# Inverse transform read back in long rows, DK reload ahead of weights and U^T, first dense blocks moved behind the first Z

## The chip, the cores and the metric

One core of a Trainium2 chip runs the whole program in one launch. The metric is device microseconds of one execution; lower is better.

## The reference

`reference` runs a gated layer forward and takes the gradient of its output against `grad_out`. With `u` of shape 2048 x 448 (positions l, channels d), N = 256 states and F = 1792 hidden units it computes:

```python
g = sigmoid((u * gate_w).sum(-1))
K[d, l] = Re sum_n C[d,n] * exp(dt[d] * A[d,n] * l) * dt[d] * B[d,n]     # l rounded to bf16
a = irfft(rfft(pad(u)) * rfft(pad(K))) [:2048] + u * Dskip               # causal convolution
b = relu(u @ w1 + b1)**2 @ w2 + b2
out = g * a + (1 - g) * b
_out, _vjp = jax.vjp(_f, u, A_re, A_im, B_re, B_im, C_re, C_im, log_dt, Dskip, w1, b1, w2, b2, gate_w)
```

Outputs are `out` and the 14 gradients. The gradient of the convolution kernel, dK, is a correlation of `u` with `g * grad_out`; it is needed only at the bf16-rounded positions, where several l share one position. From dK come the gradients of A, B, C and dt, by sums over powers of exp(dt A).

## The kernel before

**Transforms.** The convolutions are FFTs in two matrix stages, with a trip through DRAM between the stages. `fwd1` and `fwd2` make the spectra of u and of g * grad_out, `cprod` their product, and `inv1p` (L292, store L296) the first inverse stage of dK. Its result goes to the scratch tensor `hd[0]`, laid out as (64 * k1 + 16 * g + 8 * hp + x, d), where g is 0 to 3, hp 0 or 1 and x 0 to 7.

**dK sum (L690 to L719).** `hd[0]` is read back into four tiles `hss` of 128 partitions x 3584 elements (two in buffer D16, two in P14). `load_hs(q)` (L319) reads, for one q, the x values 2q and 2q+1 of all four g: four rows of 1792 bytes per partition. SP issues the half hp = 1 and ACT the half hp = 0. Then 160 matmuls (L713) with 32-column weights from `ct["Ew"]` and `Ew2` add the terms into five PSUM tiles (and one row of a sixth). A key (x8, g, e, gr) says which x and g a matmul reads, which PSUM tile e it adds to, and which 32-partition strip gr of it: `tile_position=(0, 32 * gr)`. The keys are sorted with x8 first, so runs of four or five matmuls for one g (and almost always gr = g) follow one another, g by g.

**DK trip (L717 to L735).** ACT copies the PSUM tiles to `stA`, `stB`. Thirteen small stores to `dk_d` alternate between the queues of SP and POOL (GpSimd). Five loads and one row on each of the two queues then read `dk_d` into `DK` (buffer K28), one copy per 64 partitions, each load waiting for the stores it reads.

**Weights.** `w1` goes to buffer U16 by three DMAs on SP (L697, L700), issued behind the `hd[0]` loads; `w2` (L1029) goes to D16 on POOL; the first two blocks of U^T (`load_ut`, L568) go to SB on POOL, behind a memset of `XB`.

**Main loop (L960 to L1006).** c runs over NCH = 14 chunks of 32 channels. `build_x` (L773, L774, L777) and `build_y` (L784, L785, L787) double tables of powers on DVE, the latter in two halves; `expand_x`, `expand_y` (L807 to L814) on ACT spread the factors they need from the loads `recx`, `recy` (L798, L802). `tables_t` and `turn_yt` transpose on PE and copy on ACT (L871, L883), `load_yt` transposes by DMA on SP (L890). `kgen` (L844) makes K. `dk_chunk(c)` (L895, L896, on ACT) copies the chunk's part of DK to `DKs`. One round later `back_z` multiplies DKs with the Y tables on PE (L913, copy L917 on ACT) and `back_p` multiplies the result Z with the X tables on DVE (L933) and sums on PE (L942). Of each half of `build_y` from c = 1 on, the second is ordered behind the first half's `back_p`.

**Dense part.** `hidden(lb, jp)` computes two 128-row blocks of the hidden layer: eight matmuls (L584, L587) from w1 and U^T, two Relu (L589) and a Square (L591) on ACT, and a store (L595). `project` (L1021, L1022) is the second layer. At the end of round c = 0 six hidden blocks are traced, into the PSUM tags NT[4:6] ("X" and "S").

**What sets the order.** Every engine runs its own instructions in a fixed order, worked out at build time from the trace order, priorities and dependencies. `tc.issue_after(ins)` adds an order edge behind `ins` on the same engine, without a wait for its completion. DMAs of one queue are issued in order.

Of the kernel before, what the change touches and what calls it, by code (L numbers as in the profile page):

```python
# [19 lines left out]
P = 128  # L20
L, D, N, F = 2048, 448, 256, 1792
# [6 lines left out]
NG = 4  # L28
# [306 lines left out]
def kernel(ctx, tc, A_u, A_A_re, A_A_im, A_B_re, A_B_im, A_C_re, A_C_im, A_log_dt, A_Dskip,  # L335
# [3 lines left out]
    nc = tc.nc  # L339
    V, S, G_, T_ = nc.vector, nc.scalar, nc.gpsimd, nc.tensor  # L340
# [9 lines left out]
    hd = [dscr(f"hd{i}", SPN) for i in range(3)]  # L350
# [5 lines left out]
    dk_d = dscr("dk_d", 769 * D)  # L356
# [10 lines left out]
    K = Ker(tc, pool, psum)  # L367
# [30 lines left out]
    for h in range(2):  # L398
        for g in range(NG):
            src = bass.AP(tensor=u2.tensor, offset=u2.offset + (16 * g + 8 * h) * D, ap=[[64 * D, 32], [1, 8 * D]])  # L400
# [65 lines left out]
    NT = ["N0", "N1", "N2", "N3", "X", "S"]  # L466
# [75 lines left out]
    e, im = (x.rearrange("p c w -> p (c w)") for x in (E0, Tt))  # L542
# [24 lines left out]
    def load_ut(lb):  # L567
        G_.dma_start(UTb[lb % 2].rearrange("p a l -> p (a l)"), bass.AP(tensor=UT_d, offset=lb * P * 2048, ap=[[2048, P], [1, 2048]]))  # L568
# [4 lines left out]
    def hidden(lb, jp, banks, ring):  # L573
        nonlocal nti, rxi
        ub = UTb[lb % 2]
        rx = ring[rxi % len(ring)]
        rxi += 1
        pss = []
        for j in (2 * jp, 2 * jp + 1):
            ps = K.ps(banks[nti % len(banks)], [P, 512])  # L580
            nti += 1
            pss.append(ps)
            for dt in range(DT - 1):
                T_.matmul(ps[:], lhsT=w1w[:, dt, j * P:j * P + P], rhs=ub[:, dt], start=(dt == 0), stop=False, skip_group_check=True)  # L584
        for k in range(2):
            h, j = slice(64 * k, 64 * k + 64), 2 * jp + k
            T_.matmul(pss[k][:], lhsT=w1w[h, 3, j * P:j * P + P], rhs=ub[h, 3], start=False, stop=True, tile_position=(64 * k, 0), skip_group_check=True)  # L587
        for k in range(2):
            S.activation(rx[:, 512 * k:512 * k + 512], pss[k][:], ACT.Relu, bias=b1_f[:, 2 * jp + k:2 * jp + k + 1])  # L589
        if jp < 6:  # L590
            S.activation(SB[:, 4096 + 1024 * jp:5120 + 1024 * jp], rx, ACT.Square)  # L591
        else:
            for k in range(2):
                S.activation(hsq(12 + k), rx[:, 512 * k:512 * k + 512], ACT.Square)
        G_.dma_start(bass.AP(tensor=rT_d, offset=2 * jp * P * L + 512 * lb, ap=[[L, P], [P * L, 2], [1, 512]]), rx.rearrange("p (k l) -> p k l", k=2))  # L595
# [14 lines left out]
    for rb, _, _ in psets:  # L610
        xs, ys, _, _ = fields(rb.rearrange("p (c r) -> p c r", c=4))
# [76 lines left out]
        Ew2 = SB[:, 10752:10752 + NW2]  # L688
        nc.sync.dma_start(Ew2, nc.inline_tensor(cs["Ew2"].astype(ml_dtypes.bfloat16), name="c_Ew2").ap())
    hsD, hsP = K.t("D16", [P, 8192]), K.t("P14", [P, 7168])  # L690
    hss = [b[:, 3584 * i:3584 * i + 3584].rearrange("p (g x d) -> p g x d", g=4, x=2) for b in (hsD, hsP) for i in range(2)]
    for q in range(4):
        lhs = K.load_hs(hd[0], q, hss[q], True)
    w1v = K.t("U16", [P, 8192])
    w1w = w1v[:, 0:7168].rearrange("p (a f) -> p a f", a=DT)
    with tc.issue_after(lhs.ins):
        nc.sync.dma_start(w1w[:, 0:3], bass.AP(tensor=B_w1.tensor, offset=B_w1.offset, ap=[[F, P], [P * F, 3], [1, F]]))  # L697
    for h in range(2):
        with tc.issue_after(lhs.ins):
            nc.sync.dma_start(w1w[64 * h:64 * h + 64, 3], bass.AP(tensor=B_w1.tensor, offset=B_w1.offset + 384 * F, ap=[[F, 64], [1, F]]))  # L700
    KB = K.t("K28", [P, 14336])
    DK = KB[:, 0:VA * D].rearrange("p (a d) -> p a d", d=D)
    G_.memset(KB[:, 12 * D:VA * D].bitcast(fp32), 0.0)
# [1 line left out]
    psE = K.psF()  # L705
    tiles = [psS[0], psS[1], psS[2], psS[3], psE[:, 0], psE[:, 1]]
    first, last = {}, {}
    for k, (x8, g, e, gr) in enumerate(ekeys):
        first.setdefault((e, gr), k)
        last[e, gr] = k  # L710
    for k, (x8, g, e, gr) in enumerate(ekeys):
        lt = ct["Ew"][:, 32 * k:32 * k + 32] if k < 128 else Ew2[:, 32 * k - 4096:32 * k - 4064]
        T_.matmul(tiles[e][32 * gr:32 * gr + 32, 0:D], lhsT=lt, rhs=hss[x8 // 2][:, g, x8 % 2, :], start=(k == first[e, gr]), stop=(k == last[e, gr]),  # L713
                  tile_position=(0, 32 * gr), skip_group_check=True)
    stA, stB = (K.t("st", [P, 4, D], bufs=2) for i in range(2))
    for i in range(4):
# [2 lines left out]
    S.copy(stB[0:1, 1], psE[0:1, 1, 0:D])  # L719
    pieces = [(2 * e, 2, 128 * e, 1, stA[:, e]) for e in range(4)] + [(8, 4, 512, 2, stB[:, 0])]  # L720
    n_ = 0
    ldk = {}
    for (a0, na, r0, st_, src) in pieces:
        for al in range(na):
            qe = (nc.sync, G_)[n_ % 2]
# [3 lines left out]
    for cpy in range(2):  # L729
        qe = (nc.sync, G_)[cpy]  # L730
        with tc.issue_after(ldk[cpy].ins):
            for (a0, na, r0, st_, _) in pieces:
                qe.dma_start(DK[64 * cpy:64 * cpy + 64, a0:a0 + na].rearrange("p a d -> p (a d)"),
                             bass.AP(tensor=dk_d, offset=r0 * D, ap=[[na * D, 64], [1, na * D]]))
            qe.dma_start(DK[64 * cpy:64 * cpy + 1, 12], bass.AP(tensor=dk_d, offset=768 * D, ap=[[D, 1], [1, D]]))  # L735


    YA = K.t("Y16", [P, W2, 2, 64])
# [2 lines left out]
    XWs = [XB[:, 4096 * k:4096 * k + 4096].rearrange("p (t w a r) -> p t w a r", t=2, w=W2, a=NA) for k in range(2)]  # L741
    for k in range(2):
        mx = G_.memset(XB[:, 4096 * k:4096 * k + 4096].bitcast(fp32), 0.0)
    with tc.issue_after(mx.ins):
        load_ut(0)
        load_ut(1)
    Fv = K.t("F17", [P, 8704])
    Vt = Fv[:, 0:4096]
    PRY = Fv[:, 4096:5376].rearrange("p (l w t d) -> p l w t d", l=5, t=2, d=2)
# [148 lines left out]
    def back_z(c, YTs, gs):  # L898

        nonlocal zi  # L900
        cc = c % GC
        DKc = DKs[:, c % 2]
        zb = Zr[zi % 2].rearrange("p (s t g n) -> p s t g n", t=2, s=2, g=2)
        zi += 1
        for gg, g in enumerate(gs):
            psz = K.psF()
            for s in range(2):
                for par in (1, 0):
                    for ii in range(4):
                        i = 2 * ii + par  # L910
                        m = (1 + par) * NA
                        for t in range(2):
                            T_.matmul(psz[32 * ii:32 * ii + m, t, 256 * s:256 * s + 256],  # L913
                                      lhsT=DKc[64 * t:64 * t + 64, s, g, 2 * ii:2 * ii + 1 + par].rearrange("p i a -> p (i a)"),
                                      rhs=YTs[g][64 * t:64 * t + 64, :, i, :], start=True, stop=True, tile_position=(64 * t, 32 * ii),
                                      skip_group_check=True)
            S.copy(zb[:, :, :, gg].rearrange("p s t n -> p t s n"), psz[:].rearrange("p t (s n) -> p t s n", s=2))  # L917
        return zb
# [46 lines left out]
    for c in range(NCH + 1):  # L965
        z01 = z23 = None
        if c < NCH:
            with tc.issue_after(ay.ins) if ay is not None else nullcontext():
                seeds_x(c)
            ax = build_x(c)  # L970
            if c + 1 < NCH:
                load_rx(c + 1)
            XTs[c] = [tables_t(c, 0)]
            YTs[c] = []
        if c > 0:
            z01 = back_z(c - 1, YTs[c - 1], (0, 1))
        if c < NCH:
            XTs[c].append(tables_t(c, 1))
        if c > 0:
            z23 = back_z(c - 1, YTs[c - 1], (2, 3))  # L980
        for half in range(2):
            if c < NCH:
                ay = build_y(c, half, ax if half == 0 else ap or ay)
                if half == 1:
                    k_out(c, kgen(c))
                for g in (2 * half, 2 * half + 1):
                    YTs[c].append(turn_yt(c, g, ("S", "N3")) if c == 0 else turn_yt(c, g) if g == 3 or c == NCH - 1 else load_yt(c, g))
                if c + 1 < NCH:
                    if half == 0:
                        lry = load_ry(c + 1)  # L990
                        lry1 = lry if c == 0 else lry1
                        expand_x(c + 1)
                        if c == 0:
                            expand_y(1, 0, 4)
                    elif c == 0:
                        expand_y(1, 4, 5)
                    else:
                        expand_y(c + 1)
                if half == 0:
                    dk_chunk(c)  # L1000
            ap = None
            if c > 0:
                ap = back_p(c - 1, XTs[c - 1][half], (z01, z23)[half], (2 * half, 2 * half + 1), ay if c < NCH else None)
        if c == 0:
            for jp in range(6):
                hidden(0, jp, NT[4:6], [w1v[:, 7168:8192], Fv[:, 2048:3072], Fv[:, 3072:4096]])  # L1006

    ring = [w1v[:, 7168:8192], Fv[:, 2048:3072], Fv[:, 3072:4096], P2[:, 0:1024], P2[:, 1024:2048]]
    ni = 0
# [15 lines left out]

    w2v = K.t("D16", [P, 8192])
    w2n = w2v[:, 0:FT * D].rearrange("p (j d) -> p j d", d=D)
    with tc.issue_after(lry1.ins):
        G_.dma_start(w2n, bass.AP(tensor=B_w2.tensor, offset=B_w2.offset, ap=[[D, P], [P * D, FT], [1, D]]))  # L1029
    hidden(0, 6, NT[0:3], ring)  # L1030
    for lb in range(4):
# [410 lines left out]
```

## Time and profile before

| | us |
|---|---|
| runs | 958.52, 960.26, 954.6, 958.17 |
| median of the four | 958.35 |
| profiled execution | 958.52 |
| its span | 956.4 |
| PE busy | 712.3 (74% of the span) |
| DVE busy | 671.3 (70%) |
| ACT busy | 586.1 (61%) |
| POOL busy | 191.7 (20%) |

The span runs from the first to the last instruction of the core; 2.1 us of the execution's time lie around it. Engines: PE is TensorE (PEld its weight loads), DVE VectorE, ACT ScalarE, POOL GpSimd, SP SyncE (here only a DMA queue). "L713" is line 713 of the kernel before. Tiles are written by the first letters of their names, so "S" can be the buffer SB or a PSUM tag, and "K<-dk_d" is the DK reload. The mean granted TensorE clock is 0.831 of full speed.

### The profile page before, as it was taken

What the parts mean: (1) busy time and instruction counts of PE and PEld (TensorE: products, weight loads), DVE (VectorE), ACT (ScalarE), POOL (GpSimd) and SP (SyncE); (2) the same over time, 40 slices, a digit from 0 to 9 for tenths busy, and PEclk for the clock granted to TensorE, in tenths of its full rate; (3) what the DMA queues carried; (4) which work ended last, traced back from release to release, by engine and by line L of the source; (5) the groups of instructions that cost most, each with busy time, mean ns of one, the idle gap of its engine ahead of it and who ended that gap; (6) DMA issues with size and microseconds to landing.
All of it is one profiled execution on the core that took longest, in us unless ns stands there. A gap on an engine that the chain in (4) does not pass through costs nothing. (4 is left out here: it accounts for less than half of the span.)

```text
span 956.4 us, 18969 instructions
## 1 busy us (share of the span) xinstructions
PE 712.3 (74%) x7625; PEld 342.8 (36%) x7657; DVE 671.3 (70%) x1152; ACT 586.1 (61%) x936; POOL 191.7 (20%) x327
## 2 busy tenths in 40 slices
PE   3346675735878888787987886988958889868975
PEld 1112222214344443344543442443323345423443
DVE  4387885786499999899986899854238662288800
ACT  3335757725997869689676755664327645437544
POOL 2141000113202122021202311232300022433310
PEclk9675555668869899899966998899968879868998
DMA  9976486797526756436843976469998995879531
GB/s 187 264 236 228 167 310 244 285 314 218 132 66 124 154 135 136 110 84 148 191 88 89 234 152 141 127 156 287 355 330 265 274 293 177 215 231 288 152 105 45
DMA packets 161887, 184.98 MB, mean 193 GB/s; under 512 B 90963, under 2 KB 137464, under 8 KB 160872
## 3 DMA queue, kind: packets, MB, share of 16 engines
q1 hardware_dynamic: 111958, 82.38, 35.4%
q0 software_dynamic: 20480, 61.51, 19.9%
q10 hardware_dynamic: 29362, 39.88, 12.9%
q8 instruction: 60, 0.98, 0.4%
q14 instruction: 27, 0.22, 0.1%
HBM read 90.58 MB, written 73.13 MB: 171 GB/s over the span
## 5 line engine op out<-in xcount | busy, mean ns | idle before, releaser
L933 DVE TENSOR_TENSOR P<-R 128x2048 bf16<-128x2048 bf16 x42 | 49.5, 1218 | 23.7 <-ACT R L917 20.9
L1159 PEld LDWEIGHTS <-S 128*128 128x128 bf16 x448 | 43.8, 103 | 60.6 <-issue 18.5
L917 ACT CAST R<-psF 128x1024 bf16<-128x1024 f32 x56 | 57.5, 1026 | 12.4 <-PE psF L913 12.4
L1021 PE MATMUL psN<-D,S 128*128 128x448 bf16 x208 | 53.5, 391 | 6.4 <-ACT S L591 6.3
L1159 PE MATMUL psF<-U,S 128*128 128x448 bf16 x224 | 51.7, 381 | 2.1 <-ACT S L1154 2.0
L913 PE MATMUL psF<-R,S 64*32 64x256 bf16 (+1 forms) x1344 | 37.9, 296 | 9.7 <-DMA R<-Y 4.6
L584 PE MATMUL psN<-S,U 128*128 128x512 bf16 x119 | 37.6, 420 | 9.7 <-ACT F L589 4.8
L1084 PE MATMUL psN<-S,U 128*128 128x512 bf16 x113 | 35.6, 425 | 8.6 <-ACT D L1089 6.9
L773 DVE TENSOR_TENSOR X<-X,F 128x512 bf16<-128x512 bf16 (+1 forms) x70 | 37.4, 534 | 4.8 <-ACT F L807 2.9
L207 DVE CAST K<-psN 128x448 bf16<-128x448 f32 x36 | 21.6, 620 | 27.2 <-PE psN L255 27.1
L1153 PEld LDWEIGHTS <-S 128*128 128x128 bf16 x448 | 30.0, 103 | 28.3 <-issue 11.6
L784 DVE TENSOR_TENSOR K<-K,F 128x2048 bf16<-128x2048 bf16 (+3 forms) x42 | 36.4, 866 | 5.4 <-ACT F L812 3.8
L1097 POOL DMA_DIRECT2D dhT_d<-D x28 | 20.2, 720 | 91.1 <-DVE D L1096 90.9
L785 DVE TENSOR_TENSOR F<-K,F 128x2048 bf16<-128x2048 bf16 (+3 forms) x42 | 35.9, 855 | 3.0 <-ACT F L814 3.0
L784 DVE TENSOR_TENSOR Y<-Y,F 128x2048 bf16<-128x2048 bf16 (+3 forms) x42 | 36.3, 864 | 1.5
L787 DVE TENSOR_TENSOR K<-K,F 128x2048 bf16<-128x2048 bf16 (+3 forms) x42 | 36.3, 865 | 1.3
L787 DVE TENSOR_TENSOR Y<-Y,F 128x2048 bf16<-128x2048 bf16 (+3 forms) x42 | 36.3, 865 | 1.3
L774 DVE TENSOR_TENSOR F<-X,F 128x512 bf16<-128x512 bf16 (+1 forms) x70 | 36.8, 526 | 0.6
L785 DVE TENSOR_TENSOR F<-Y,F 128x2048 bf16<-128x2048 bf16 (+3 forms) x42 | 35.9, 854 | 0.3 <-ACT F L814 0.3
L1021 PE MATMUL psN<-S,D 128*128 128x448 bf16 x168 | 35.7, 361 | 0.0
L1354 DVE SCALAR_TENSOR_TENSOR F<-psN,Y 128x448 bf16<-128x448 f32 x16 | 9.9, 618 | 36.0 <-PE psN L329 36.0
L883 ACT COPY M<-psX 128x1024 bf16<-128x1024 bf16 x26 | 26.6, 1022 | 14.0 <-PE psX L882 13.9
(378 smaller groups left out, 1946.7 us busy)
## 6 DMA issues: line engine op xcount, KB each, us to landing
sp<-K ACTq DMA_DIRECT2D x8, 896.0 KB, 8.5
hd<-st ACTq DMA_DIRECT2D x16, 448.0 KB, 2.9
dhT_d<-D POOLq DMA_DIRECT2D x28, 256.0 KB, 5.2
R<-sp SPq DMA_DIRECT2D x8, 896.0 KB, 9.1
S<-rT_d POOLq DMA_DIRECT2D x14, 512.0 KB, 5.3
R<-hd SPq DMA_DIRECT2D x16, 448.0 KB, 6.1
S<-dhT_d POOLq DMA_DIRECT2D x14, 512.0 KB, 4.5
rec_d<-F ACTq DMA_DIRECT2D x2, 1920.0 KB, 9.1
```

The costliest lines, as they stand in the source:

```text
L584: T_.matmul(ps[:], lhsT=w1w[:, dt, j * P:j * P + P], rhs=ub[:, dt], start=(dt == 0), stop=False, skip_group_check=True)
L773: V.tensor_tensor(out=hi4, in0=lo, in1=bcast_dims(pr, [0, (None, n), 1]), op=ALU.mult)
L774: V.tensor_tensor(out=Vv.rearrange("p (x a r) -> p x a r", x=2 * W2, r=2), in0=lo, in1=bcast_dims(pi, [0, (None, n), 1]), op=ALU.mult)
L784: V.tensor_tensor(out=hi, in0=lo, in1=bcast_dims(pr, [0, (None, n // 2), 1]), op=ALU.mult)
L785: V.tensor_tensor(out=Vv.rearrange("p (x a q) -> p x a q", x=rows, q=2), in0=lo, in1=bcast_dims(pi, [0, (None, n // 2), 1]), op=ALU.mult)
L787: return V.tensor_tensor(out=T4[:, :, :, n:2 * n], in0=T4[:, :, :, n:2 * n], in1=V4, op=ALU.add)
L913: T_.matmul(psz[32 * ii:32 * ii + m, t, 256 * s:256 * s + 256], lhsT=DKc[64 * t:64 * t + 64, s, g, 2 * ii:2 * ii + 1 + par].rearrange("p i ...
L917: S.copy(zb[:, :, :, gg].rearrange("p s t n -> p t s n"), psz[:].rearrange("p t (s n) -> p t s n", s=2))
L933: lastp = V.tensor_tensor(out=pr.rearrange("p s t g n -> p s t (g n)"), in0=zv, in1=(xb if r == 0 else rev_dim(xb, 2)), op=ALU.mult)
L1021: lastm = T_.matmul(ps[:, 0:D], lhsT=hblk[j][:, P * tt:P * tt + P], rhs=ws[:, j, :], start=(w == 1 and j == 0), stop=(j == FT - 1))
L1084: T_.matmul(ps[:], lhsT=w2Tw[:, jp, dt, j % 2], rhs=dblk[:, dt], start=(dt == 0), stop=False, skip_group_check=True)
L1159: lastm = T_.matmul(ps[:, 0:width], lhsT=hh[:, t, :], rhs=(DB2[:, t, :] if w == 0 else U[:, t, 0:D + 1]), start=(t == 0), stop=(t == LT - 1))
```

## The change

Line numbers up to the first hunk are those of before; later ones move by -3 to +4.

1. The `hd[0]` reload is cut by g instead of by q. One load for a g and an hp takes all eight x: one row of 7168 bytes per partition instead of four of 1792. The bytes, the queues and the number of DMAs stay.
2. The 160 matmuls are sorted by g first and x8 second (`eorder`). All matmuls of g = 0 now come ahead of those of g = 1, and so on.
3. The three w1 loads move on SP from behind the `hd[0]` loads to behind the DK reload; U^T (POOL) moves to behind POOL's DK reload, and the order edge of w2 (POOL) goes to the same place.
4. The six early hidden blocks are traced in round c = 1 behind `back_z(0)`, and into the PSUM tags NT[0:3] instead of NT[4:6].
5. In round 0 `dk_chunk(0)` is traced in the second half instead of the first.

The number of instructions stays the same on every engine. In the built program the order differs from before only from the `hd[0]` loads to the early part of round c = 3; from there to the end the orders on all five engines are identical. On PE, L584 of the first early hidden block now stands between the two halves of `back_z(0, (0, 1))`.

```diff
-    hss = [b[:, 3584 * i:3584 * i + 3584].rearrange("p (g x d) -> p g x d", g=4, x=2) for b in (hsD, hsP) for i in range(2)]
-    for q in range(4):
-        lhs = K.load_hs(hd[0], q, hss[q], True)
+    hss = [b[:, 3584 * i:3584 * i + 3584].rearrange("p (x d) -> p x d", d=D) for b in (hsD, hsP) for i in range(2)]
+    for g in range(NG):
+        for hp in range(2):
+            src = bass.AP(tensor=hd[0], offset=(16 * g + 8 * hp) * D, ap=[[64 * D, 64], [1, 8 * D]])
+            lhs = (nc.scalar if hp == 0 else nc.sync).dma_start(hss[g][64 * hp:64 * hp + 64].rearrange("p x d -> p (x d)"), src)
     w1v = K.t("U16", [P, 8192])
     w1w = w1v[:, 0:7168].rearrange("p (a f) -> p a f", a=DT)
-    with tc.issue_after(lhs.ins):
-        nc.sync.dma_start(w1w[:, 0:3], ...)
-    for h in range(2):
-        with tc.issue_after(lhs.ins):
-            nc.sync.dma_start(w1w[64 * h:64 * h + 64, 3], ...)
...
+    eorder = sorted(range(len(ekeys)), key=lambda k: (ekeys[k][1], ekeys[k][0]))
-    for k, (x8, g, e, gr) in enumerate(ekeys):
+    for k in eorder:
+        x8, g, e, gr = ekeys[k]
         lt = ct["Ew"][:, 32 * k:32 * k + 32] if k < 128 else Ew2[:, 32 * k - 4096:32 * k - 4064]
-        T_.matmul(..., rhs=hss[x8 // 2][:, g, x8 % 2, :], ..., tile_position=(0, 32 * gr), ...)
+        T_.matmul(..., rhs=hss[g][:, x8, :], ..., tile_position=(0, 32 * gr), ...)
...
+            lrk[cpy] = qe.dma_start(DK[64 * cpy:64 * cpy + 1, 12], ...)
+    with tc.issue_after(lrk[0].ins):
+        nc.sync.dma_start(w1w[:, 0:3], ...)
+        for h in range(2):
+            nc.sync.dma_start(w1w[64 * h:64 * h + 64, 3], ...)
+    with tc.issue_after(lrk[1].ins):
+        load_ut(0)
+        load_ut(1)
...
-    with tc.issue_after(mx.ins):
-        load_ut(0)
-        load_ut(1)
...
             z23 = back_z(c - 1, YTs[c - 1], (2, 3))
+        if c == 1:
+            for jp in range(6):
+                hidden(0, jp, NT[0:3], [w1v[:, 7168:8192], Fv[:, 2048:3072], Fv[:, 3072:4096]])
...
-                if half == 0:
+                if half == (1 if c == 0 else 0):
                     dk_chunk(c)
...
-        if c == 0:
-            for jp in range(6):
-                hidden(0, jp, NT[4:6], [w1v[:, 7168:8192], Fv[:, 2048:3072], Fv[:, 3072:4096]])
...
-    with tc.issue_after(lry1.ins):
+    with tc.issue_after(lrk[1].ins):
         G_.dma_start(w2n, ...)
```

## The prediction

> **What bounds the kernel now.** All edits lie between the `hd[0]` reload and round c = 3, so I read the busy times of each engine by stage first (columns: length, busy us of PE, PEld, DVE, ACT, POOL, granted clock, DMA share, GB/s).
>
> ```profile
> 196.00:206.70 10.70, 0.00 (x0) 0.00 (x0) 9.93 (x20) 2.51 (x4) 2.13 (x4) 0.50 0.92 281
> 206.70:220.30 13.60, 11.17 (x162) 6.06 (x163) 13.22 (x19) 1.97 (x4) 1.66 (x2) 0.86 1.05 327
> 220.30:237.20 16.90, 10.59 (x200) 8.31 (x200) 11.75 (x21) 9.43 (x15) 6.76 (x12) 0.82 0.72 211
> 237.20:242.90 5.70, 1.95 (x10) 1.20 (x10) 3.57 (x3) 5.30 (x9) 0.00 (x0) 0.50 0.15 40
> 242.90:256.30 13.40, 12.47 (x114) 5.07 (x114) 0.05 (x2) 12.42 (x18) 2.87 (x4) 0.93 0.45 113
> 256.30:267.00 10.70, 8.44 (x181) 4.39 (x182) 8.78 (x10) 10.70 (x15) 2.04 (x4) 1.00 0.99 207
> 267.00:300.00 33.00, 28.12 (x529) 15.93 (x524) 32.04 (x51) 26.26 (x38) 3.62 (x7) 0.74 0.45 92
> ```
>
> From 267 on DVE is 97% busy and sets the pace. Before it DVE idles 13.35 us at a stretch; the question is when DVE can go through with X(2). The waits of 196 to 262 (who waits for whom, total us, times, longest) give the chain that leads there:
>
> ```profile
> PE psN L713 <- DMA D<-hd: 15.5, 1, 15.5
> DVE P L933 <- ACT R L917: 13.4, 1, 13.4
> ACT S L895 <- DMA K<-dk_d: 5.8, 1, 5.8
> POOL K L733 <- DMA dk_d<-st: 4.2, 1, 4.2
> DVE K L784 <- ACT F L812: 3.8, 1, 3.8
> SPq L733 <- DMA dk_d<-st: 2.8, 2, 1.5
> ```
>
> `hd[0]` reload, 160 matmuls (L713), stores, DK reload, `dk_chunk` (L895), ACT's queue, L917, DVE. Its stations in the timeline:
>
> ```profile
> 206.73 1.34 PE L713 MATMUL psN<-D,M 128*32 128x448 bf16 x12 [15.48 <-DMA D<-hd]
> ...
> 208.20 1.37 PE L713 MATMUL psN<-D,M 128*32 128x448 bf16 x12
> ...
> 211.09 0.78 PE L713 MATMUL psN<-D,M 128*32 128x448 bf16 x12
> 211.65 0.40 PE L713 MATMUL psF<-D,M 128*32 128x448 bf16 x4
> ...
> 237.17 0.89 ACT L895 COPY S<-K 128x416 bf16<-128x416 bf16 x1 [5.79 <-DMA K<-dk_d]
> ...
> 266.95 0.42 DVE L774 TENSOR_TENSOR F<-X,F 128x512 bf16<-128x512 bf16 x1
> ```
>
> Four dates therefore fix the sum: PE starts L713 at 206.73, ends it at 220.25, DK has landed at 237.17, DVE passes L774 of X(2) at 266.95. From there the order is that of before on DVE, and PE, ACT have slack, so a shift of L774 is the shift of the whole.
>
> **Reload, start of L713.** 3.67 MB (8 x 448 KB) stay. Rows of 7168 bytes gain little: the reload already runs at 327 GB/s with the DMA share at 1.05; the page's fastest slice has 355, so at most 1 us, hidden behind PE below. U^T (2 x 512 KB) leaves this stretch: 1.05 MB at 281 GB/s is 3.7 us, and w1's issue at 205.5 came too late to delay the first pair. L713 starts at 206.7 - 3.7 = 203.0. Bounds: 206.7 if the U^T share was not what held the first pair; 201.5 if the pair, issued at 197.0, needs only its 2.8 us (0.92 MB at 327 GB/s) and the 1.7 us in which the smallest `t_d<-st` (16 KB) lands.
>
> **L713 itself.** The rows above hold 16 matmuls in 208.20 - 206.73 = 1.47 us with PE just woken (four for each 32-column strip, 0.37 us a step), and 0.56 us from the first to the fourth step (0.19 each) once it runs at full clock from about 210. So four strips run at the same time and one strip takes one matmul per 0.19 us. In the order of before, four or five matmuls of a strip follow one another and the next strip's stand right behind them, which PE evidently reaches: 160 x 0.19 / 4 = 7.6 us of work, waiting for data most of its 13.5 us. The new order puts the 39 to 43 matmuls of one g together, and counted from the keys 32 of them go to the strip of that g. How far does PE look past a blocked strip? The last 42 and 54 matmuls before show it: L713 there took 2.33 us (212.64 to 214.96) and 2.9 us (217.01 to 219.90) to its last start; replayed with a queue of four matmuls per strip and the issue stopped when that queue is full, their keys give 2.31 and 2.93; with three 3.31 and 3.39, with six or more 2.08 and 2.65. Four it is. Then g = 0 to 3 hardly overlap: 4 x 32 x 0.189 = 24.2 us, less three hand-overs of three matmuls, 1.7, is 22.5 us. The slow first 3.3 us cost 1.7 more: 24.2 us, behind which the later loads (the last at about 212) are hidden. L713 ends at 203.0 + 24.2 = 227.2, 7.0 later than before. Bounds: 215 with unlimited look-ahead (the last load, then its own 3 us), 229 with none.
>
> A rule to weigh here: the Trainium skill's "TensorE: Matmul & The Clock Gate", section "The mechanism", has matmuls start and end strictly in program order. The rows contradict it, since matmul 13 starts 0.04 us after matmul 1 and ahead of 2. By the rule both orders would be nearly serial and the new one would end at 229.
>
> **End of L713 to DK.** 16.9 us before: copies and stores (3.6 to the last issue), waiting for the stores to land (SP 2.8, POOL 4.2), ten issues of 0.54 us, landing. Stores of POOL and SP stood in their queues behind w2 (1568 KB, 14.4 us to landing) and w1 (15.8 us). With these gone the stores land about as `s_d<-st` and `t_d<-st` do, 1.7 to 2.3 us, while the queue still issues the others; the first reload goes out 3.3 us (POOL) and 4.0 us (SP) after L713 instead of 7.3 and 6.8. I take 3.4 us off: 13.5, DK at 240.7. Bounds: 4.2 off; only 1 off if w1 and U^T, now right behind the reload, slow it (the stretch already has 0.72 of the DMA for 211 GB/s). `dk_chunk(0)` behind `expand_y` costs nothing, and removes DVE's 3.8 us wait for L812, which lay inside the 13.35 us idle time: hidden either way.
>
> **DK to L774.** 29.8 us before, nearly all of it ACT in a row: from 237.2 to 267 it is busy 28.4. The change moves the six hidden blocks (12 Relu of 0.58, 6 Squares of 0.95, 12.7 us) behind the first L917, so DVE's first L933 comes at about DK + 12 instead of + 19. But ACT must still pass all of them ahead of the second L808, without which L774 can't run. ACT's list from L895 to that L808: 3 dk copies 2.6, L852 0.3, four L883 3.6, four L917 3.6, two L871 1.8, two L807 and two L808 2.1, 12 Relu 6.9, five Squares 4.75: 25.6 us. To it come 1.4 us of waits for PE between the L883 (0.56 + 0.82 before) and a new wait: `recx` of round 2 is now issued on SP behind w1, and an L807 that needs it stands ahead of the second L917. 1.79 MB of w1 share the DMA with U^T and w2 (2.7 MB) at some 330 GB/s from DK - 1 on: w1 done at DK + 9.8, `recx` at + 11, against a need at DK + 9. Wait 2 us; bounds 0 and 6. Also PE's L584, which now stands between the halves of z01, waits for w1's first 1.34 MB (DK + 7 against + 6). Sum 29.0 us: L774 at 240.7 + 29.0 = 269.7, 2.7 us later than before.
>
> **Sum.** 7.0 (L713) - 3.4 (stores) - 0.8 (ACT) = +2.8 us on the profiled execution's 958.5, which stands 0.2 above the median: 961.
>
> **Rivals.**
> *Overlap after all.* PE looks further past a blocked strip than I infer, and L713 is bound by data: end at 215 to 218, -5 to -2 instead of +7, everything behind it unchanged: 949 to 952. For it: in the first stretch four strips ran together. Against: the replay fits at four within 0.03 us.
> *The weights arrive late.* Slower. One mechanism: SP's queue brings `recx` only behind w1, and ACT, in order, holds L917 for it. w1 landed 15.8 us after its issue before, under load; now issued about DK - 6, that is DK + 10, its last piece and `recx` DK + 14: a wait of 5 instead of 2, and PE's L584 holds z01 for the same data, so up to 4 more for DK, whose last rows share the queues. 964 to 969. It decides once `recx` lands later than DK + 12. For it: POOL and SP hold 6.2 MB behind L713's end, against 1.75 MB before.
> *No net effect.* L774 stays within 1 us of 266.95, since start and stores give what L713 takes: 957.5 to 960.
>
> **How the numbers follow.** About 0.5% (4.8 us) is what a measurement can tell from no change. Forecast, 959 to 963: 0.35. No net effect: 0.15. Late weights: 0.35, nearly all above 963.2. Overlap: 0.15, nearly all below 953.6. That gives faster 0.15, same 0.5, slower 0.35. The range leaves out a tenth at each side: 951 reaches into the overlap case, 969 ends the late weights.
>
> **What would show it.** Right: L713 runs 22 to 26 us with one strip at a time, its matmuls 0.19 us apart, starting at 202 to 204; SP's and POOL's wait for `dk_d<-st` under 2 us; DVE's first L933 about 12 us after L895, a second idle time ahead of L773 or L774 of X(2), and ACT without a gap but for L807. Wrong: L713 under 18 us (my look-ahead is wrong), or L895 more than 16 us after its end (the reload is not freed but crowded), or ACT idle ahead of L807 by over 4 us.

## The result and the profile after

The changed kernel takes 961.19 us (median of 37 runs, 954.23 to 968.97) against 953.8 for the kernel before (58 runs, 941.94 to 961.59). The ratio is 1.0099 with a 95% interval of 1.008 to 1.0117: slower by 7.6 to 11.2 us. The ratio leaves out runs more than 1.5% above the fastest of their kernel, which is why it says more than the 7.4 us between the two medians; the executions profiled for e1 and e10 below are such runs, and only dates up to X(2) are read from them. The four runs shown beforehand had a median of 958.35, which is 4.5 above that of the 58. The profiled execution after took 961.9 (span 959.9, granted clock 0.839), the one before 958.5 (span 956.4).

The lines of the changed kernel: L713 stays, the dk copies L895 and L896 are L899 and L900, L913 and L917 of `back_z` are L917 and L921, DVE's products L933 and their sums L942 are L937 and L946, L774 is L778, L870 and L871 of `tables_t` are L874 and L875. The stages after, with the columns of the prediction's first view (length, busy us of PE, PEld, DVE, ACT, POOL, granted clock, DMA share, GB/s):

```profile
194.30:201.30 7.00, 0.00 (x0) 0.00 (x0) 6.59 (x15) 3.44 (x6) 0.55 (x1) 0.50 0.90 210
201.30:225.60 24.30, 24.25 (x163) 12.17 (x164) 19.54 (x29) 1.16 (x3) 0.53 (x1) 0.94 0.47 113
225.60:238.80 13.20, 7.82 (x192) 7.09 (x190) 7.68 (x12) 9.87 (x16) 8.88 (x15) 0.86 0.78 221
...
242.90:256.00 13.10, 8.35 (x90) 4.49 (x90) 0.06 (x1) 6.74 (x9) 0.00 (x0) 0.52 1.02 222
256.00:271.40 15.40, 14.01 (x256) 6.45 (x257) 8.88 (x10) 15.40 (x23) 3.84 (x6) 1.00 0.64 155
```

The L713 stage has grown from 13.6 to 24.3 us, and PE is busy in all of it. The store and reload stage behind it shrank from 16.9 to 13.2. From 242.9 to 256.0 ACT is busy 6.74 us, where it was busy 12.42 before: it waits, at a DMA share of 1.02. The waits from 194 to 272 (who waits for whom, total us, times, longest):

```profile
ACT st L717 <- PE psN L713: 22.8, 1, 22.8
DVE P L937 <- ACT R L921: 13.2, 1, 13.2
...
DVE K L788 <- ACT F L816: 7.7, 1, 7.7
...
ACT R L875 <- PE psX L874: 5.5, 1, 5.5
...
DVE P L937 <- PE psN L946: 4.8, 1, 4.8
PE psN L584 <- DMA U<-in_B_w_dram: 4.5, 1, 4.5
...
ACT S L899 <- DMA K<-dk_d: 3.3, 1, 3.3
```

Neither SP's nor POOL's wait for the stores of `dk_d` is in the list any more. New are PE's wait for w1 (L584), ACT's for PE behind it (L875) and DVE's for L946. New as well is DVE's 7.7 us for ACT's first `expand_y` (L816), which stands in ACT's order behind the late copies of L713; it lies ahead of DVE's 13.2 us idle time, which hides it. The stations in the timeline (start, us, engine, line, operation; in brackets the idle time ahead and what ended it):

```profile
201.35 1.30 PE L713 MATMUL psN<-D,M 128*32 128x448 bf16 x3 [12.71 <-DMA D<-hd]
...
211.69 0.35 PE L713 MATMUL psN<-D,M 128*32 128x448 bf16 x1
...
211.87 0.35 PE L713 MATMUL psF<-D,M 128*32 128x448 bf16 x1
...
212.06 0.35 PE L713 MATMUL psN<-D,M 128*32 128x448 bf16 x1
...
238.87 0.90 ACT L899 COPY S<-K 128x416 bf16<-128x416 bf16 x1 [3.27 <-DMA K<-dk_d]
...
250.25 0.61 PE L584 MATMUL psN<-S,U 128*128 128x512 bf16 x1 [4.53 <-DMA U<-in_B_w_dram]
...
255.94 1.22 DVE L937 TENSOR_TENSOR P<-R 128x2048 bf16<-128x2048 bf16 x1 [13.17 <-ACT R L921]
...
268.01 1.22 DVE L937 TENSOR_TENSOR P<-R 128x2048 bf16<-128x2048 bf16 x1 [4.84 <-PE psN L946]
...
271.40 0.43 DVE L778 TENSOR_TENSOR F<-X,F 128x512 bf16<-128x512 bf16 x1 [1.43 <-ACT F L812]
```

The middle rows show single matmuls 0.18 to 0.19 us apart, where before sets of four started together. This execution reached the `hd[0]` reload 2.6 us earlier than the profile before (first issue at 194.38 instead of 196.96), ahead of all that was changed but the issue of U^T, which came 0.8 us before that reload. So all dates below are counted from the first issue of that reload. X(2) stands for DVE's first pass of L778 (before: L774) for X(2), the last station of the prediction: +70.0 before, +77.0 after.

### The profile page after: what moved, and what is told of

Same layout as the page of the kernel before. It is cut to its first block, busy times and chain, and to the rows that moved or that the text cites. A ratio compares the mean times of both kernels' runs of the same rounds, so it can differ in the third digit from the quotient of the medians.

```text
span 959.9 us, 18973 instructions
## 1 busy us (share of the span) xinstructions
PE 721.5 (75%) x7625; PEld 347.5 (36%) x7657; DVE 671.2 (70%) x1152; ACT 586.2 (61%) x936; POOL 191.8 (20%) x327
## 3 DMA queue, kind: packets, MB, share of 16 engines
q10 hardware_dynamic: 28594, 39.88, 12.9%
## 4 chain that ended last, share of the span: by engine, by line
PE 29%; DMA 20%; ACT 19%; issue 14%; DVE 12%; POOL 3%; SPq 2%; ACTq 1%; POOLq 0%; DVEq 0%
PE psN L1025 5%; PE psF L1163 3%; ACT R L921 3%; DMA S<-rT_d 2%; PE psX L848 2%; PE psN L584 2%; DMA R<-Y 2%; PE psN L1088 2%; DMA U<-in_B_w_dram 2%; PE psN L713 2%; SPq L422 2%; DMA R<-K 2%; DMA hd<-st 1%; PE psX L886 1%; ACT R L875 1%
## 5 line engine op out<-in xcount | busy, mean ns | idle before, releaser
L937 DVE TENSOR_TENSOR P<-R 128x2048 bf16<-128x2048 bf16 x42 | 49.6, 1218 | 28.5 <-ACT R L921 18.9
L921 ACT CAST R<-psF 128x1024 bf16<-128x1024 f32 x56 | 57.5, 1027 | 15.5 <-PE psF L917 12.8
L584 PE MATMUL psN<-S,U 128*128 128x512 bf16 x151 | 47.0, 411 | 14.6 <-DMA U<-in_B_w_dram 4.5
L1163 PE MATMUL psF<-U,S 128*128 128x448 bf16 x224 | 48.9, 366 | 2.4 <-ACT S L1158 2.4
L917 PE MATMUL psF<-R,S 64*32 64x256 bf16 (+1 forms) x1344 | 37.7, 296 | 13.0 <-DMA R<-Y 4.9
L1088 PE MATMUL psN<-S,U 128*128 128x512 bf16 x113 | 36.2, 432 | 7.4 <-ACT D L1093 5.4
L207 DVE CAST K<-psN 128x448 bf16<-128x448 f32 x36 | 21.6, 619 | 25.2 <-PE psN L255 25.0
L778 DVE TENSOR_TENSOR F<-X,F 128x512 bf16<-128x512 bf16 (+1 forms) x70 | 36.9, 526 | 2.0 <-ACT F L812 1.4
L917 PEld LDWEIGHTS <-S 64*16 64x16 bf16 (+1 forms) x1792 | 22.3, 90 | 38.6 <-issue 24.4
L789 DVE TENSOR_TENSOR F<-Y,F 128x2048 bf16<-128x2048 bf16 (+3 forms) x42 | 35.8, 853 | 0.0
L887 ACT COPY M<-psX 128x1024 bf16<-128x1024 bf16 x26 | 26.7, 1026 | 14.7 <-PE psX L886 13.9
## 6 DMA issues: line engine op xcount, KB each, us to landing
dhT_d<-D POOLq DMA_DIRECT2D x28, 256.0 KB, 5.1
```

The costliest lines, as they stand in the source:

```text
L778: V.tensor_tensor(out=Vv.rearrange("p (x a r) -> p x a r", x=2 * W2, r=2), in0=lo, in1=bcast_dims(pi, [0, (None, n), 1]), op=ALU.mult)
L789: V.tensor_tensor(out=Vv.rearrange("p (x a q) -> p x a q", x=rows, q=2), in0=lo, in1=bcast_dims(pi, [0, (None, n // 2), 1]), op=ALU.mult)
L937: lastp = V.tensor_tensor(out=pr.rearrange("p s t g n -> p s t (g n)"), in0=zv, in1=(xb if r == 0 else rev_dim(xb, 2)), op=ALU.mult)
L1088: T_.matmul(ps[:], lhsT=w2Tw[:, jp, dt, j % 2], rhs=dblk[:, dt], start=(dt == 0), stop=False, skip_group_check=True)
L1163: lastm = T_.matmul(ps[:, 0:width], lhsT=hh[:, t, :], rhs=(DB2[:, t, :] if w == 0 else U[:, t, 0:D + 1]), start=(t == 0), stop=(t == LT - 1))
```

## The experiments

Each was profiled once, and all but the last also timed against the kernel before (e4 with 6 runs, the others with 12). "DK" is the first dk copy on ACT, "product" DVE's first product with Z. Dates in us from the first issue.

| kernel | L713 from, to | DK | product | X(2) | ratio (95%) |
|---|---|---|---|---|---|
| before | 9.8, 23.3 | 40.2 | 59.3 | 70.0 | |
| changed | 7.0, 31.1 | 44.5 | 61.6 | 77.0 | 1.0099 (1.008 to 1.0117) |
| e1, old order | 6.9, 28.2 | 44.1 | 58.1 | 70.5 | 1.0034 (0.9999 to 1.0069) |
| e3, w1 early | 7.2, 32.9 | 45.2 | 57.3 | 72.8 | 0.9987 (0.9947 to 1.0026) |
| e4, blocks back | 7.5, 33.0 | 46.1 | 72.4 | 83.1 | 1.013 (1.0079 to 1.0181) |
| e5, rows and order alone | 10.8, 35.8 | 47.9 | 67.1 | 77.8 | 1.0076 (1.0045 to 1.0107) |
| e2, old rows and order | 7.2, 20.7 | 36.5 | 51.6 | 67.0 | 0.9979 (0.9947 to 1.0011) |
| e8, e2 with w1, U^T early | 7.1, 21.6 | 45.3 | 52.9 | 63.9 | 1.0008 (0.9977 to 1.004) |
| e6, e8 with blocks ahead of DK | 7.3, 21.8 | 53.0 | 61.1 | 70.3 | 0.9962 (0.9921 to 1.0003) |
| e9, before with blocks ahead of DK | 9.5, 23.4 | 53.5 | 61.6 | 70.8 | 1.0005 (0.9963 to 1.0048) |
| e11, edits 4 and 5 alone | 10.1, 23.5 | 40.5 | 51.4 | 64.2 | 1.0025 (0.9978 to 1.0072) |
| e7, e2 with w1 early | 7.3, 21.8 | 34.7 | 46.8 | 62.2 | 0.9974 (0.9936 to 1.0011) |
| e10, e7 with blocks later | 7.3, 21.7 | 34.5 | 46.6 | 62.7 | 0.9997 (0.9946 to 1.0048) |
| e12, order by pairs of g | 7.0, 28.5 | 43.0 | 57.8 | 73.2 | one run, 952.98 us |

An edit at one place can also change the order that the build works out for the engines behind it.

**e1, the order of the matmuls.** On the changed kernel:

```diff
-    eorder = sorted(range(len(ekeys)), key=lambda k: (ekeys[k][1], ekeys[k][0]))
+    eorder = list(range(len(ekeys)))
```

> The changed kernel with the 160 matmuls back in the order x first, g second; loads stay in rows of 7168 bytes, one tile per g, so the first four matmuls already need all of them. Dates are counted from the issue of the first reload. In the changed kernel the L713 matmuls run from +7.0 to +31.1. Theory (column strips serialise): the matmuls wait for the last load, about +18 by the DMA packets of the changed kernel's trace, then take 8 to 10 us, four strips at once: end +26 to +28, about 4 us before the changed kernel's, and all behind it moves along; ratio to before about 1.005 instead of 1.010. Rival (L713 is long because its data come late in long rows): first matmul at +18 too, but the last stays at about +31 and the ratio at 1.010.

In the timeline of e1 PE works off the first few matmuls of each tile as it lands, and then all strips at once:

```profile
212.83 0.55 PE L713 MATMUL psN<-P,M 128*32 128x448 bf16 x1 [0.62 <-DMA P<-hd]
...
217.04 0.35 PE L713 MATMUL psN<-P,M 128*32 128x448 bf16 x1
...
217.06 0.37 PE L713 MATMUL psN<-D,M 128*32 128x448 bf16 x2
...
217.08 0.36 PE L713 MATMUL psF<-D,M 128*32 128x448 bf16 x1
```

The last tile is there at 212.83 (+18.8). Each tile holds one g, and in the order x first the matmuls of the first x already need all four tiles. The 145 matmuls left then take 9.4 us to the end of the last, 0.065 us each against 24.15 / 160 = 0.151 in the changed kernel; four start within 0.04 us. L713 ends 2.9 us earlier than in the changed kernel although it must wait for all the data, X(2) comes 6.5 earlier, and the ratio falls from 1.0099 to 1.0034. For L713 the theory held (+28.2 against +26 to +28), and the rival fell. But the rest did not simply move along: DK comes 15.9 us behind L713 instead of 13.4, so that only 0.4 us is left there, and the other 6.2 us lie between DK and X(2). There ACT already has four L887 copies behind it (from 232.54 on, ahead of DK at 238.13), which the changed kernel runs behind DK (from 241.62 on).

**e3, w1 early.** On the changed kernel, the three w1 loads behind `lhs` on SP again:

```diff
+    with tc.issue_after(lhs.ins):
+        nc.sync.dma_start(w1w[:, 0:3], ...)
...
-    with tc.issue_after(lrk[0].ins):
-        nc.sync.dma_start(w1w[:, 0:3], ...)
```

> The changed kernel with w1 issued on SP right behind the reload, as before, instead of behind the DK reload; U^T and w2 stay late. Theory (late w1 holds PE's L584 and so DVE's second pair of products): w1 lands while the matmuls L713 run, PE's 4.5 us wait for w1 goes, X(2) passes DVE's last step at about DK + 28 instead of DK + 32.5, 4 us gained: ratio about 1.006. Rival (the place of the dense blocks is what costs, w1's wait lies beside it): DK + 32 as in the changed kernel, ratio 1.010. Third: U^T, now alone behind the DK reload, is the later one, and the wait just changes its name.

The timeline of e3 from the dk copy (L899) on:

```profile
239.36 0.93 ACT L899 COPY S<-K 128x416 bf16<-128x416 bf16 x1 [2.47 <-DMA K<-dk_d]
...
251.49 2.36 DVE L937 TENSOR_TENSOR P<-R 128x2048 bf16<-128x2048 bf16 x2 [7.45 <-ACT R L921]
...
263.56 1.23 DVE L937 TENSOR_TENSOR P<-R 128x2048 bf16<-128x2048 bf16 x1 [4.84 <-PE psN L946]
...
266.95 0.43 DVE L778 TENSOR_TENSOR F<-X,F 128x512 bf16<-128x512 bf16 x1 [1.43 <-ACT F L812]
```

PE's wait for w1 is gone, and with it ACT's 5.45 us ahead of L875. The first product comes at DK + 12.1 instead of DK + 17.1, X(2) at DK + 27.6 instead of DK + 32.5. The ratio falls to 0.9987, by more than the 4.2 us of the date. DVE's 4.84 us wait for L946 stays: w1 did not cause it. For U^T and w2, still late, PE waits nowhere for over 1 us up to X(2).

**e4, the blocks back.** On the changed kernel, the six blocks at the end of round c = 0 with banks `NT[4:6]`, as before:

```diff
-        if c == 1:
-            for jp in range(6):
-                hidden(0, jp, NT[0:3], ...)
...
+        if c == 0:
+            for jp in range(6):
+                hidden(0, jp, NT[4:6], ...)
```

> The changed kernel with the six dense blocks back at the end of round c = 0 and in their old banks; reload, order of the matmuls, weights and dk_chunk as changed. Theory (late w1 is the cost, and moving the blocks behind the first Z hid part of it): the blocks wait for w1 until about DK + 11.4 and ACT reaches the copies of Z only behind them, X(2) at DK + 36 to 40: ratio 1.014 to 1.018. Rival (the place of the blocks ahead of L946 costs): X(2) at about DK + 29, ratio 1.006.

The timeline of e4: PE meets w1 now in a bank that the transposes for Y need too, and ACT waits for them.

```profile
249.99 1.46 PE L584 MATMUL psX<-S,U 128*128 128x512 bf16 x3 [9.41 <-DMA U<-in_B_w_dram]
...
252.34 1.01 ACT L887 COPY M<-psS 128x1024 bf16<-128x1024 bf16 x1 [8.43 <-PE psS L886]
```

DK + 37.0 for X(2), 6.0 us later than in the changed kernel. Edit 4 is no cost here but hides part of the late w1. The rival fell. (The ratio's interval still holds that of the changed kernel.)

**e5, edits 1 and 2 alone** on the kernel before (long rows, g first):

```diff
-    for q in range(4):
-        lhs = K.load_hs(hd[0], q, hss[q], True)
+    for g in range(NG):
+        for hp in range(2):
...
-    for k, (x8, g, e, gr) in enumerate(ekeys):
+    eorder = sorted(range(len(ekeys)), key=lambda k: (ekeys[k][1], ekeys[k][0]))
+    for k in eorder:
```

> The kernel before with the long rows and the g-first order alone; weights, U^T and dense blocks as before. Theory (strips serialise): L713 takes 24 us also here and ends at about +31 to +34 from the first issue (before +23.3). By then w1 and w2 have landed, so that the stores of dk run free also without the moved weights: 13.5 us instead of 16.9 from the last matmul to DK, then 29.8 us to X(2) as before: 4.4 to 7.2 us more, ratio 1.005 to 1.0075. Rival (order and rows are harmless, the moved weights and blocks cost): ratio 1.000 and L713 ending at about +23. Third: if the stores still wait 4 us for w1 and w2, ratio 1.008 to 1.011, and the moved weights are what frees them.

L713 takes 25.1 us and ends at +35.8; DK follows 12.1 us behind its end, without any weight moved. X(2) is 7.8 later than before, the ratio 1.0076. So the order and the rows alone make a loss of this size. They are not all that counts: e3, whose L713 ends nearly as late (+32.9), comes out at 0.9987. Its X(2) is 5.0 us earlier than that of e5, from which it differs by edits 4 and 5 and by the late U^T and w2. The third case fell as well: once L713 lasts that long, w1 and w2 have landed by themselves, and moving them frees nothing.

**e2, edits 1 and 2 taken back** on the changed kernel:

```diff
-    for g in range(NG):
-        for hp in range(2):
...
+    for q in range(4):
+        lhs = K.load_hs(hd[0], q, hss[q], True)
...
-    eorder = sorted(range(len(ekeys)), key=lambda k: (ekeys[k][1], ekeys[k][0]))
+    eorder = list(range(len(ekeys)))
```

> The changed kernel with both the rows of 1792 bytes (one load for two x of all four g) and the order x first taken back; weights, dense blocks and dk_chunk stay as changed. Dates from the issue of the first reload. With long rows and the old order (the run before this one) L713 ended at +28.2. Theory A (long rows load more slowly): the short rows bring the data in by about +18 and the last matmul ends at +20 to +22, DK at about +34, X(2) past DVE's last step at +61 to +65 (before +70.0): ratio 0.991 to 0.997. Rival (the rows make no difference, only the order does): L713 ends at about +28 again, ratio 1.003.

L713 ends at +20.7, 7.5 us earlier than in e1. Only 1.9 us of that is the speed of the load: the last tile is there at +16.9 instead of +18.8. The other 5.6 us come from how the tiles are cut: with two x of all four g in a tile, PE works ahead in the order x first, and 70 matmuls are left behind the last tile instead of 145. (Part of it may be the granted clock, which was 0.50 until +22.4 in e1 and until +16.2 in e2.) So theory A's dates came true, but its reason covers a quarter of the gain. The two kernels' windows from 2 us after the first issue to the last tile (columns as above) show the rate of all transfers, e1 first, e2 second:

```profile
196.00:212.80 16.80, 7.20 (x23) 2.48 (x23) 16.28 (x22) 5.40 (x8) 0.55 (x1) 0.50 0.92 225
```

```profile
196.50:211.38 14.88, 8.40 (x90) 4.18 (x93) 13.92 (x20) 2.40 (x4) 0.55 (x1) 0.52 0.97 259
```

225 GB/s in rows of 7168 bytes, 259 in rows of 1792. DK came 15.8 us behind L713, later than the 13 to 14 that I had counted on, and PE waited 2.6 us for w1, so X(2) at +67.0 missed what I expected by 2. The ratio, 0.9979, is just above what I expected.

**e8, U^T and w1 behind the reload on SP**, w2 late, blocks behind the first Z; on e2:

```diff
+    with tc.issue_after(lhs.ins):
+        load_ut(0, nc.sync)
+        load_ut(1, nc.sync)
+        nc.sync.dma_start(w1w[:, 0:3], ...)
...
-    with tc.issue_after(lrk[0].ins):
-        nc.sync.dma_start(w1w[:, 0:3], ...)
...
-    with tc.issue_after(lrk[1].ins):
-        load_ut(0)
-        load_ut(1)
```

> Short rows, old order, and U^T and w1 behind the reload on SP instead of behind the DK reload; w2 stays behind the DK reload, the dense blocks behind the first Z. Theory: U^T and w1 land at about +20 to +24, before PE needs them; L713 ends at +20 to +23, DK at +34 to +37, PE does not wait for w1, X(2) at DK + 27.6 as in the run with w1 early: +62 to +64, ratio about 0.993. Rival (w1 and U^T in SP's queue hold the stores of dk, the DK reload comes as late as before, +40): X(2) at +68, ratio 0.998 to 1.000.

X(2) at +63.9 as expected, but by another way: with w1 and U^T early the first Relu of a block already ran at +27.2, ACT came to the dk copies only at +45.3, and X(2) followed 18.6 us behind them. The ratio, 1.0008, shows nothing of the 6 us.

**e6, the blocks ahead of dk_chunk(0)**, on e8, and **e9**, the same move on the kernel before (the lines are those of e9; in e6 the blocks come from behind the first Z):

```diff
-                if half == 0:
+                if half == 0 and c > 0:
                     dk_chunk(c)
...
         if c == 0:
             for jp in range(6):
-                hidden(0, jp, NT[4:6], ...)
+                hidden(0, jp, NT[0:3], ...)
+            dk_chunk(0)
```

> As the kernel with U^T and w1 early, but the six dense blocks stand ahead of dk_chunk(0), so that PE and ACT work them off while the DK reload is under way. Theory: ACT idles there otherwise; most of the 12.7 us of Relu and Square leave the stretch between DK and X(2). DVE's first product at about DK + 10, X(2) at +56 to +59 instead of +70: ratio 0.985 to 0.990. Rival (the blocks stand ahead of the copies that Y(1) needs, DVE's Y(1) comes later by as much): ratio 0.995 to 1.000.

> The kernel before with one thing changed: the six dense blocks (banks NT[0:3]) stand ahead of dk_chunk(0). Nothing of the change is in it. Theory: DK lands at +40 as before, the blocks lie ahead of it, X(2) at about DK + 18 to 20, +58 to +60 instead of +70: ratio 0.987 to 0.992. Rival (w1 and U^T arrive too late for them, at about +24 to +28, and they hold ACT's queue until after DK): ratio 0.998 to 1.003.

Both theories fell. ACT is in order: it passes the dk copies only at +53 behind nearly all the blocks, although the reload was issued at +27 and +31. X(2) stays at +70.3 and +70.8, no interval leaves out 1. That is e9's rival (1.0005, and the blocks hold ACT's queue until after DK). In e6 the ratio lies in its rival's range, but not for its reason: the last step of the first half of Y(1) starts at +38.2, against +38.0 in e8.

**e11, edits 4 and 5 alone** on the kernel before:

```diff
+        if c == 1:
+            for jp in range(6):
+                hidden(0, jp, NT[0:3], ...)
...
-                if half == 0:
+                if half == (1 if c == 0 else 0):
                     dk_chunk(c)
...
-        if c == 0:
-            for jp in range(6):
-                hidden(0, jp, NT[4:6], ...)
```

> The kernel before with edit 4 (dense blocks behind the first Z, dk_chunk(0) behind expand_y) alone; loads, order of the matmuls and weights as before. Dates from the issue of the first reload. Theory: DK at +40 as before; w1 is there, so PE does not wait for it, and X(2) follows at DK + 27.6 as in the run with w1 early, +68 instead of +70: ratio 0.996 to 1.000. Rival (the place of the blocks costs, through DVE's wait for L946): X(2) at DK + 32, +72, ratio 1.002 to 1.005.

X(2) came at DK + 23.7, even earlier than I expected, and DVE's wait for L942 is 2.7 us. Here the first three Relu already run from +30.7 on, ahead of DK (before: from +48.8). So with w1 in time the new place of the blocks is good for X(2). But the ratio, 1.0025 (0.9978 to 1.0072), shows no gain.

**e7, w1 early, short rows, old order**, U^T and w2 late, blocks behind the first Z. The edit on e2 is that of e3 on the changed kernel:

```diff
+    with tc.issue_after(lhs.ins):
...
-    with tc.issue_after(lrk[0].ins):
         nc.sync.dma_start(w1w[:, 0:3], ...)
```

> Short rows, old order and w1 behind the reload on SP as before; U^T and w2 behind the DK reload and dense blocks behind the first Z as changed. Theory: L713 ends at +21, DK 12.3 us behind it as in the run with w1 early (+33 to +34), X(2) at DK + 27.6: +61 to +62 against +70: ratio 0.990 to 0.993. Rival (the reload of DK is still crowded by U^T and w2, 15.8 us as in the run with short rows, old order and late w1): X(2) at +64, ratio 0.994 to 0.997.

DK comes 12.9 us behind L713 (e2: 15.8), X(2) at DK + 27.6 = +62.2, the earliest of all. The dates are as the theory has them, the ratio of 0.9974 (0.9936 to 1.0011) is not: all of 0.990 to 0.993 lies outside. It beats the changed kernel, whose interval begins at 1.008. That it beats the kernel before is not shown.

**e10, the blocks at the end of round c = 1**, behind both `back_p`, on e7:

```diff
         if c == 1:
             for jp in range(6):
-                hidden(0, jp, NT[0:3], [w1v[:, 7168:8192], Fv[:, 2048:3072], Fv[:, 3072:4096]])
+                hidden(0, jp, NT[0:3], [w1v[:, 7168:8192], P2[:, 0:1024], P2[:, 1024:2048]])
```

> The kernel above with the six dense blocks moved on, to the end of round c = 1, and their ring of buffers partly in M8 instead of F17. Theory: DVE's 4.8 us wait for PE's L946, which stood behind the blocks, goes, and ACT has 12.7 us less ahead of X(2): X(2) at DK + 22 to 24, +55 to +58, ratio 0.984 to 0.988, if PE and ACT find room for the blocks in rounds c = 2 to 4. Rival (PE has no room there and the rounds get longer by what was gained): X(2) early, but ratio as of the kernel above.

```profile
DVE P L935 <- PE psN L944: 7.3, 1, 7.3
```

This line of e10's waits was 4.8 in e7. The first block still reached ACT at +50.2 (e7: +47.6): the order worked out at build time had put blocks ahead of these sums again, and PE came to most of the sums even later. How much of that is the order is not shown: from 244 to 250 the granted clock was 0.50 in this execution, 0.96 to 1.00 in that of e7. X(2) and the ratio stay. What the blocks would cost wholly behind the sums was not tried.

**e12, pairs of g.** On the changed kernel:

```diff
-    eorder = sorted(..., key=lambda k: (ekeys[k][1], ekeys[k][0]))
+    eorder = sorted(..., key=lambda k: (ekeys[k][1] // 2, ekeys[k][0], ekeys[k][1]))
```

> The changed kernel with the matmuls sorted by pairs of g (0 and 1 interleaved by x, then 2 and 3), everything else as changed. Theory (one strip works off one matmul per 0.189 us, with a queue of four per strip): two strips run at a time, the replay gives 14.3 us of PE time instead of 22.5; with the tiles landing at +6.9, +11.5, +16.2 and +18.8 (seen in the run with the old order alone) and some 1.7 us for a slow start, L713 ends at +26 to +28 instead of +31.1. Rival (the g-first order is slow for its reads of one tile, not for its strips): first pair and second pair 12 us each, end at +31 to +36.

```profile
215.98 0.37 PE L713 MATMUL psN<-P,M 128*32 128x448 bf16 x2
...
216.17 0.37 PE L713 MATMUL psN<-P,M 128*32 128x448 bf16 x2
...
216.36 0.37 PE L713 MATMUL psF<-P,M 128*32 128x448 bf16 x2
```

Two at a time, 0.19 us apart, and L713 ends at +28.5, half a microsecond above what the theory gave and 2.5 below the rival's lower end. In three kernels with the same loads (the changed one, e12, e1) one, two and four strips run at a time. The tiles that are read change along with the strips here; that it is the strips shows in the kernel before, where the first 16 matmuls, four at a time (the prediction's rows from 206.73 on), all read one tile. So the strip theory is shown.

## Why the prediction was right and wrong

The predicted time, 961.0, is the measured median to 0.2 us, and that is partly luck. It was +2.8 us on an execution of 958.5, which stood 4.7 us above the median of the 58. The change costs 7.4 us by the medians and 953.8 x 0.0099 = 9.4 us by the ratio, so it was taken 4.6 to 6.6 us too small, and the two errors nearly cancel. By the prediction's own bound of 0.5% the likeliest class, no change, was wrong; slower, with a chance of 0.35, holds.

- **Start of L713.** Forecast at +6.0 (203.0 - 196.96), measured +7.0. U^T's share held the first pair, as assumed.
- **Rows.** "Gain little" was right for the changed kernel only because PE hid them. In themselves they lose a little: the last tile came at +18.8 (e1) instead of +16.9 (e2). That L713 ends 7.5 us later in e1 than in e2 is for the greater part the cut by g.
- **Length of L713.** Forecast 24.2 us, measured 24.15, one strip at a time and 0.19 us a step, for the reason given: e1 and e12 change the number of strips at work and get the time for it. The rule on program order from the Trainium skill ("TensorE: Matmul & The Clock Gate", section "The mechanism") would have had all three orders nearly serial; e1 took 0.065 us a matmul behind its last tile, the changed kernel 0.151. That page's table in the section "Why this matters for your kernels" gives 2.38 times for three column groups at once; here four gave 0.151 / 0.065 = 2.3 times with the slow clock at e1's start, and 0.189 / 0.05 = 3.8 times in e1's last 108 matmuls, at the full granted clock.
- **L713 to DK.** Forecast 13.5, measured 13.4, and the waits of SP and POOL for the stores are gone. But that is luck in part, and the credit goes to the wrong edit: e5 has 12.1 us with all weights at their old place, and with a short L713 the moved weights save only 1.1 us (15.8 in e2, 16.9 before), not the forecast 3.4. The longer L713 gave w1 and w2 time to land, and w1 right behind the reload slows it: with w1 early it takes 12.3 instead of 13.4 (e3 against the changed kernel) and 12.9 instead of 15.8 (e7 against e2).
- **DK to X(2).** This step failed: forecast 29.0 us (-0.8), measured 32.5 (+2.7). The term mis-sized is PE's wait in L584, put at "DK + 7 against + 6" and in effect at nothing; w1 let PE go on at DK + 11.4, 17.3 us after its first issue at 232.95, and its last piece landed 18.5 us after its own issue (15.8 before, the figure in the rival). I had looked for the wait at ACT's L807 through `recx`, 2 us. `recx` did land late, at DK + 14.2, but ACT, held at L875 until then, came to L811 (before: L807) only 0.4 us after that, so it cost nothing more. PE stood 4.5 us in the blocks between the halves of z01, ACT lost 5.45 us ahead of L875, and e3 gives the sum: without the wait DK + 27.6. DVE's first product came at DK + 17.1 instead of the forecast 12. Not seen at all was DVE's 4.84 us behind L946, which PE runs behind blocks that wait for ACT.
- **The rivals.** *Late weights* held as a mechanism, by its second half, PE's L584. Its mark, `recx` later than DK + 12, came true too (DK + 14.2), but ACT did not wait for `recx`, so it was the wrong one to watch; its time, 964 to 969, did not come. *Overlap after all* and *no net effect* fell.
- **Sum.** By dates the steps make +7.8 (end of L713), -3.5 (to DK), +2.7 (to X(2)): +7.0 at X(2), of 7.6 to 11.2 by the ratio.

**What stays open.** The prediction took a shift of L774 for a shift of the whole. Losses at X(2) do show in the times: +7.0, +7.8 and +13.1 against 9.4, 7.2 and 12.4 us from the ratios of the changed kernel, e5 and e4. Most gains don't: e7, e8, e10 and e11 have -7.8, -6.1, -7.3 and -5.8 at X(2) and -2.5, +0.8, -0.3 and +2.4 by the ratios, each to about 3 to 5 us either way (e2 agrees: -3.0 and -2.0). That the profile of before reached X(2) later than usual is not borne out from the reload on: L713's start and end (+9.8, +23.3) come again in e9 and e11 (9.5 and 10.1, 23.4 and 23.5), DK (+40.2) in e11 (40.5), DK to X(2) (29.8) in e5 (29.9). Nor did these executions give all of the gain back at once: from X(2) to X(4) it is 55.6 us before, 55.5 in e7, and 1 to 2 us more in e8, e10 and e11 (57.3, 56.7, 57.7). From X(2) to the end of the span it is 689.4 us before and 689.7, 688.2 and 688.1 in e7, e8 and e11. But e2, e4, e6, e9 and e12 have 682.6 to 686.6 there, so one execution of each settles nothing to better than several us. Where the gain goes stays open.

## What to carry to other kernels

Matmuls that write different 32-column strips run side by side only when they stand close together in PE's order; sorting them by the operand that lands first can put one strip's matmuls in a row and cost more than the wait for data that it saves. When a load is moved behind a critical one, look for every instruction on an in-order engine that reads it, and for the critical work that now stands behind that instruction: here a dense block between two halves of Z. And a transfer that a long stage hides is free in that stage only: take the stage away, and its own time, its cut into tiles and the place of the weights decide.

## What the runs showed of the hardware

- Per 32-column strip PE worked off one 448-wide matmul per 0.189 us at full clock, four strips side by side; a replay with a queue of four matmuls per strip, and the issue stopped when one is full, gave 22.5 us and with the slow start 24.2 for the g-first order (measured 24.15).
- The same 3.67 MB had come in 18.8 us after the first issue in rows of 7168 bytes (e1; 18.4 to 19.1 in the changed kernel, e4 and e12) and 16.9 us after it in rows of 1792 (e2), at 225 and 259 GB/s of all transfers (e1, e2), on the same queues with the same number of DMAs. Why the long rows are slower is not shown; the tiles are also cut differently.
- w1 (1792 KB), issued behind the DK reload with U^T and w2 on the way, let PE go on only 17.3 us after its first issue; the DMA share was 1.02 from 242.9 to 256.0.
